# Block-balanced attention into expert routing: another layout for the block balancing, another order for the first loads

## The chip, the cores and the metric

The kernel runs on one core of one Trainium2 chip. The metric is the device time of one execution in microseconds (us).

## The reference, cut to what matters

Two layers are computed one after the other. The first is attention on 4 batches of 8 heads, with 768 positions of 64 numbers. For each batch and head an 8 by 8 matrix is balanced (five times: exponential, rows divided by their sums, columns divided by their sums), and the eight blocks of 96 keys and values are mixed with it before each block of queries attends to its block.

```python
P = sort_net                                   # 4, 8, 8, 8
for _ in range(5):
    P = P - np.max(P, axis=-1, keepdims=True)
    P = np.exp(P)
    P = P / (np.sum(P, axis=-1, keepdims=True) + 1e-09)
    P = P / (np.sum(P, axis=-2, keepdims=True) + 1e-09)
k_sorted = np.einsum('bhij,bhjcd->bhicd', P, k_b)
v_sorted = np.einsum('bhij,bhjcd->bhicd', P, v_b)
...                                            # softmax(q k^T / 8) v, block by block
x = attn_out                                   # 3072 rows of 512
# second layer: all 8 experts for every row, weighted by a balanced 3072 by 8 matrix
P = np.exp(x @ w_gate - max); 8 times: rows and columns divided by their sums
out += P[:, e:e + 1] * (np.maximum(x @ w1[e], 0.0) @ w2[e])    # for e in 0..7
```

## The kernel before, in words

The kernel is written in a framework that derives the waits from the data and may reorder instructions of an engine; an instruction wrapped in `pin` keeps its place behind everything that was written before it for its engine. All TensorE work is pinned, and so are nearly all loads, which GpSimd issues (`load_batch`, `load_rest` L67 to L77, `load_w1`, `load_w2`), since they convert f32 into bf16. These loads go through one queue in their order.

The first stage is the subject here. The 32 matrices lie on 32 partitions as P, 64 numbers each (L59). The balancing (L108 to L124) runs on VectorE alone, but for the exponentials on ScalarE. The result is written 16 times over as Prep (L126), turned by eight products with an identity into Pb (L352 to L354), and multiplied by a mask into R (`build_r`, L136): one 128 by 128 matrix per head, with which TensorE mixes the blocks. `sort_values` (L149) does this for the values of a batch and then exchanges partitions: eight DMAs (four issued by SP, four by GpSimd, L159 to L163) copy `vs` to `vsb`.

Loads are issued in this order: the first batch by halves (queries, values, keys of heads 0 to 3, then of heads 4 to 7, L94), the router's weights, the second batch's values (L97), then the four exchange pieces of GpSimd, and, behind a small copy that waits until the exchange has landed (`held`, L361 to L367), the first expert's weights w1 and w2 and the second batch's keys and queries.

`attention(bb, ...)` (L263) goes through a plan of steps: q queries are transposed, k keys mixed, s scores and their exponentials, m the mix with the values, t the output turned, l the router's logits, v one part (two heads) of the next batch's values, and wN N products that nothing reads (`warm`, L341). The digit is the pair of heads. For batch 0 the queries of pairs 0 and 1 are transposed before the balancing is done (L347). PSUM has seven banks in turn for all of this.

After batch 0, `attention` of the next batch is woven with `expert0` of the batch before (L385 to L409); twelve steps of the expert stand ahead of batch 1's attention (L388 to L390). Behind the last batch come the other seven experts, about 550 us of the span, which the change does not touch.

Of the kernel before, what the change touches and what calls it, by code (L numbers as in the profile page):

```python
# [13 lines left out]
F32 = mybir.dt.float32  # L14
BF16 = mybir.dt.bfloat16
AF = mybir.ActivationFunctionType
AX = mybir.AxisListType
ALU = mybir.AluOpType


def mkap(t, dims, off=0):
    return bass.AP(tensor=t.tensor, offset=t.offset + off, ap=dims)
# [3 lines left out]
def kernel(  # L26
# [11 lines left out]
    nc = tc.nc  # L38
# [17 lines left out]
    sp = actx.enter_context(tc.tile_pool(name="sp", bufs=3))  # L56


    P = pp.tile([32, 8, 8], F32)  # L59
    nc.sync.dma_start(out=P, in_=sort_net.rearrange("b h i j -> (b h) i j"))  # L60

    pin = tc.keep_in_program_order
    kt, vt, qt = {}, {}, {}
# [1 line left out]
    def load_batch(bb, parts):  # L67
        for d, name in ((vt, "vt"), (kt, "kt"), (qt, "qt")):
            d[bb] = kvp.tile([128, 8, 384], BF16, name=name, bufs=2)
        load_rest(bb, parts)  # L70
# [11 lines left out]
    def load_w1(e):  # L82
        w1t[e] = wp.tile([128, 4, F], BF16, name="w1e")
        pin(nc.gpsimd.dma_start(out=w1t[e],
                                in_=moe_w1[e].rearrange("(kk k) f -> k kk f", k=128)))
# [5 lines left out]

    Ibig = ones.tile([128, 128], BF16)
    make_identity(nc, Ibig)
    load_batch(0, [(x, l0, 4) for l0 in (0, 4) for x in "qvk"])  # L94
    wg = ones.tile([128, 4, E], BF16)
    nc.gpsimd.dma_start(out=wg, in_=moe_w_gate.rearrange("(kk k) e -> k kk e", k=128))
    load_batch(1, [("v", 0, 8)])  # L97
    mask16 = ones.tile([128, 16], F32)
    nc.vector.reduce_sum(out=mask16, in_=Ibig.rearrange("p (j c) -> p c j", c=16), axis=AX.X)

    VW = NB * 520
    vsbt = [perp.tile([128, VW], BF16, name=f"vsb{n}") for n in range(2)]
    vs = vsp.tile([128, 6, 8, 65], BF16)
    nc.vector.memset(vs[:, :, :, 64:65], 1.0)

    rs = pp.tile([32, 8], F32)  # L108
    cs = pp.tile([32, 8], F32)
    Pt = P.rearrange("p i j -> p j i")  # L110
    nc.vector.reduce_max(out=rs, in_=P, axis=AX.X)
    nc.vector.tensor_sub(P, P, mkap(rs, [rs.ap[0], rs.ap[1], [0, 8]]))
    for it in range(5):


        nc.scalar.activation(out=P, in_=P, func=AF.Exp)
        nc.vector.reduce_sum(out=rs, in_=P, axis=AX.X)
        nc.vector.reciprocal(out=rs, in_=rs)
        nc.vector.tensor_mul(P, P, mkap(rs, [rs.ap[0], rs.ap[1], [0, 8]]))
        nc.vector.reduce_sum(out=cs, in_=Pt, axis=AX.X)  # L120
        if it == 0:
            nc.vector.tensor_scalar_add(cs, cs, 1e-9)
        nc.vector.reciprocal(out=cs, in_=cs)
        nc.vector.tensor_mul(Pt, Pt, mkap(cs, [cs.ap[0], cs.ap[1], [0, 8]]))  # L124

    Prep = perp.tile([32, 8, 8, 16], BF16)  # L126
    for eng, i0 in ((nc.vector.tensor_copy, 0), (nc.scalar.copy, 4)):
        eng(Prep[:, i0:i0 + 4], mkap(P, [P.ap[0], [8, 4], [1, 8], [0, 16]], off=i0 * 8))

    xtT = xtp.tile([128, 4, N], BF16)  # L130
    osbl = xtp.tile([128, NT, Dm], F32)
# [1 line left out]
    Pb = perp.tile([128, 32, 8], F32)  # L133
    Rt = {}

    def build_r(bb, eng, n):  # L136

        Rt[bb] = perp.tile([128, 8, 8, 16], BF16, name=f"R{bb % 2}")
        for h in range(0, 8, n):
            ins = eng.tensor_tensor(  # L140
                out=mkap(Rt[bb], [Rt[bb].ap[0], [16, 8 * n], [1, 16]], off=h * 128),
                in0=mkap(Pb, [Pb.ap[0], [1, 8 * n], [0, 16]], off=(bb * 8 + h) * 8),
                in1=mkap(mask16, [mask16.ap[0], [0, 8 * n], [1, 16]]),
                op=ALU.mult)
            if eng is nc.gpsimd:
                pin(ins)


    def sort_values(bb, bank):  # L149
        for h in range(8):  # L150
            vps = bank([128, 384], F32)
            pin(nc.tensor.matmul(vps, Rt[bb][:, h].rearrange("p i c -> p (i c)"),
                                 vt[bb][:, h, :], start=True, stop=True))
            (nc.vector.tensor_copy if bb == 0 and h % 2 else nc.scalar.copy)(
                vs[:, :, h, 0:64], vps.rearrange("p (kk d) -> p kk d", d=64))
            if h % 2:
                yield

        for i in range(NB):  # L159
            eng = nc.gpsimd if i % 2 else nc.sync  # L160
            (pin if bb == 0 else lambda ins: ins)(eng.dma_start(
                out=mkap(vsbt[bb % 2], [[VW, 96], [1, 520]], off=i * 520),
                in_=vs[16 * i:16 * i + 16].rearrange("p kk h d -> p kk (h d)")))  # L163
# [3 lines left out]
    def queries(bb, hp, bank):  # L167

        qps = bank([128, 6, 128], BF16)
        if bb < 2:  # L170

            for kk in range(6):
                for h in range(2):
                    pin(nc.tensor.matmul(qps[64 * h:64 * h + 64, kk, :],
                                         qt[bb][:, 2 * hp + h, kk * 64:kk * 64 + 64],
                                         Ibig, is_transpose=True, start=True, stop=True))
        else:
            qr = sp.tile([128, 6, 2, 64], BF16, name="qr", bufs=2)
            nc.gpsimd.tensor_copy(
                qr.rearrange("p kk h d -> p h kk d"),  # L180
                qt[bb][:, 2 * hp:2 * hp + 2].rearrange("p h (kk d) -> p h kk d", d=64))
            for kk in range(6):
                pin(nc.tensor.matmul(qps[:, kk, :], qr[:, kk].rearrange("p h d -> p (h d)"),
                                     Ibig, is_transpose=True, start=True, stop=True))
        qT[bb, hp] = sp.tile([128, 128, 6], BF16, name="qTs", bufs=4)
        nc.scalar.copy(qT[bb, hp], qps.rearrange("p kk c -> p c kk"))
# [76 lines left out]
    def attention(bb, bank, values=None, warm=None):  # L263
        first = bb == 0

        def step(what, hp):
            if what == "q":
                queries(bb, hp, bank)
            elif what == "k":
                keys(bb, hp, bank)  # L270
            elif what == "s":
                scores(bb, hp, bank)
            elif what == "t":
                turn(bb, hp, bank, nc.scalar.copy if first else nc.vector.tensor_copy)
            elif what == "l":
                logits(bb, bank, (0, 1, 2) if hp == 0 else (3,))
            elif what == "v":
                next(values, 0)
            elif what == "w":
                warm(hp)  # L280
            else:
                for h in range(2):
                    mix(bb, hp, h, bank)

        plan = ("k0 k1 w4 s0 q2 k2 w2 s1 q3 k3 w3 s2 w4 s3 w3 m0 w3 m1 t0 v0 w3 m2 t1 v0 w3 "
                "m3 t2 v0 v0 w3 t3 l0 w3 l3 v0" if first else
                "q0,q1,k0 k1,s0,q2 k2,s1,q3 m0 k3,s2 m1,t0 s3 m2,t1 m3 t2 t3,l0 l3")
        for some in plan.split():
            for x in some.split(","):
                step(x[0], int(x[1]))  # L290
            yield
# [43 lines left out]
    with tc.tile_pool(name="ps0", bufs=7, space=bass.MemoryType.PSUM,  # L335
                      reuse_waits="tile") as ps0, \
            tc.tile_pool(name="psw", bufs=1, space=bass.MemoryType.PSUM) as psw:
        bank0 = lambda shape, dt: ps0.tile(shape, dt, name="bank", tag="bank")
        unread = psw.tile([128, 4, 128], F32)

        def warm(n):  # L341

            for _ in range(n):
                pin(nc.tensor.matmul(unread, Ibig, mkap(Ibig, [Ibig.ap[0], [0, 4], [1, 128]]),
                                     start=True, stop=True))

        for hp in range(2):  # L347
            queries(0, hp, bank0)
        warm(9)
        pbps = bank0([128, 8, 32], F32)  # L350
        for i in range(8):
            pin(nc.tensor.matmul(pbps[:, i, :], Prep[:, i].rearrange("p j c -> p (j c)"),  # L352
                                 Ibig[0:32, 0:32], start=True, stop=True))
        nc.vector.tensor_copy(Pb, pbps.rearrange("p i g -> p g i"))  # L354
        build_r(0, nc.vector, 2)
        warm(4)
        for _ in sort_values(0, bank0):
            pass
        build_r(1, nc.gpsimd, 4)

        held = pp.tile([96, 2], BF16)  # L361
        gate = nc.gpsimd.tensor_copy(
            held, mkap(vsbt[0], [[VW, 96], [520, 2]], off=6 * 520 + 519))
        with tc.issue_after(gate.ins):
            load_w1(0)
            load_w2(0)
            load_rest(1, [(x, l0, 4) for l0 in (0, 4) for x in "kq"])  # L367
        for _ in attention(0, bank0, sort_values(1, bank0), warm):
            pass

# [424 lines left out]
```

## Time and profile before

| | |
|---|---|
| three runs | 685.52 to 685.59 us, median 685.56 us |
| profiled execution | 686.2 us; span from first to last instruction 684.4 us |
| granted TensorE clock, mean | 0.997 |
| PE busy | 658.6 us (96% of the span) |
| VectorE, ScalarE, GpSimd busy | 473.4, 375.4, 444.3 us |
| read from HBM, written | 52.45 MB, 6.29 MB |

In lines of the profile, PE is TensorE, PEld its weight loads, DVE VectorE, ACT ScalarE, POOL GpSimd, SP SyncE. A timeline line has the start in us, the duration in us, the engine, the line of the kernel, the operation with the names of the tiles written and read, shapes, the number of instructions merged, and in brackets how long the engine had been idle and what it waited for. A line by stretches has the stretch, then the busy time of PE, PEld, DVE, ACT and POOL with instruction counts in brackets, the granted clock, the DMA share and the GB/s that the DMA engines wrote. A line of the chain of waits has the start, the duration and what ran.

### The profile page before, as it was taken

What the parts mean: (1) busy time and instruction counts of PE and PEld (TensorE: products, weight loads), DVE (VectorE), ACT (ScalarE), POOL (GpSimd) and SP (SyncE); (2) the same over time, 40 slices, a digit from 0 to 9 for tenths busy, and PEclk for the clock granted to TensorE, in tenths of its full rate; (3) what the DMA queues carried; (4) which work ended last, traced back from release to release, by engine and by line L of the source; (5) the groups of instructions that cost most, each with busy time, mean ns of one, the idle gap of its engine ahead of it and who ended that gap; (6) DMA issues with size and microseconds to landing.
All of it is one profiled execution on the core that took longest, in us unless ns stands there. A gap on an engine that the chain in (4) does not pass through costs nothing.

```text
span 684.4 us, 13128 instructions
## 1 busy us (share of the span) xinstructions
PE 658.6 (96%) x5011; PEld 428.7 (63%) x5088; DVE 473.4 (69%) x977; ACT 375.4 (55%) x725; POOL 444.3 (65%) x417
## 2 busy tenths in 40 slices
PE   5989999999999999999999999999999999999996
PEld 2646666644446666666666666666666666666665
DVE  6627555578656777777777777777777777777775
ACT  3746646345667765555555555555555555555540
POOL 4542324201929888959797887879796979846640
PEclk9999999999999999999999999999999999999998
DMA  9898833403040304030303021030403040000223
GB/s 147 167 215 127 142 75 63 63 0 62 0 63 1 62 1 62 2 62 1 62 2 57 6 39 24 4 61 1 63 1 61 1 62 1 2 1 36 88 100 148
DMA packets 31904, 36.57 MB, mean 53 GB/s; under 512 B 2016, under 2 KB 24288, under 8 KB 31840
## 3 DMA queue, kind: packets, MB, share of 16 engines
q0 software_dynamic: 26400, 27.82, 25.4%
q1 hardware_dynamic: 5440, 7.90, 3.4%
q8 instruction: 40, 0.66, 0.4%
q14 instruction: 24, 0.20, 0.1%
HBM read 52.45 MB, written 6.29 MB: 86 GB/s over the span
## 4 chain that ended last, share of the span: by engine, by line
PE 87%; DVE 5%; DMA 4%; issue 2%; ACT 1%; POOL 1%; SPq 0%; DVEq 0%; ACTq 0%; POOLq 0%
PE oacc L631 35%; PE bk L508 34%; PE bank L306 4%; PE bank L299 4%; DMA qt<-in_q_dram 3%; PE oacc L597 2%; PE bank L232 1%; PE bk L597 1%; DVE hT L497 1%; DMA vsb<-vs 1%; PE bank L215 1%; PE bank L196 1%; PE bank L243 1%; DVE cs L484 0%; PE bk L299 0%
## 5 line engine op out<-in xcount | busy, mean ns | idle before, releaser
L581 DVE SCALAR_TENSOR_TENSOR osbl<-oacc,glog,osbl 128x256 f32<-128x256 f32 (+1 forms) x398 | 214.6, 540 | 131.8 <-PE oacc L631 114.0
L494 ACT ACTIVATE hT<-bk 128x512 bf16<-128x512 f32 x162 | 96.7, 597 | 143.1 <-PE bk L508 133.2
L508 PE MATMUL bk<-xtT,w1e 128*128 128x512 bf16 x478 | 144.3, 379 | 1.9 <-ACT hT L494 0.7
L631 PEld LDWEIGHTS <-hs 128*128 128x128 bf16 x936 | 91.6, 98 | 59.8 <-issue 0.3
L621 POOL TENSOR_TENSOR hs<-hT 128x512 bf16<-128x512 bf16 x78 | 90.5, 1160 | 48.8 <-DVE hT L497 43.3
L631 PEld LDWEIGHTS <-hT 128*128 128x128 bf16 x860 | 84.1, 98 | 55.9 <-issue 1.5
L631 PE MATMUL oacc<-w2e,hT 128*128 128x256 bf16 x752 | 112.8, 273 | 1.4 <-DVE osbl L581 1.0
L631 PE MATMUL oacc<-w2e,hs 128*128 128x256 bf16 x648 | 97.2, 273 | 0.6
L508 PE MATMUL bk<-xc,wc 128*128 128x512 bf16 x319 | 96.3, 379 | 0.0
L621 POOL TENSOR_TENSOR hs<-hT,hs 128x512 bf16<-128x512 bf16 x78 | 90.0, 1154 | 6.1
L621 POOL TENSOR_TENSOR hs<-hs,hT 128x512 bf16<-128x512 bf16 x78 | 90.0, 1154 | 6.1
L508 PEld LDWEIGHTS <-w1e 128*128 128x128 bf16 x672 | 65.8, 98 | 18.4 <-issue 4.6
L497 DVE CUSTOM_DVE_ANT_0 hT<-bk,p 128x512 bf16<-128x512 f32 x90 | 62.2, 691 | 10.2 <-PE bk L508 3.0
L553 ACT COPY p<-bk 128x512 f32<-128x512 f32 x84 | 49.2, 585 | 26.6 <-PE bk L508 23.9
L547 ACT COPY u<-bk 128x512 f32<-128x512 f32 x84 | 49.2, 586 | 24.8 <-PE bk L508 22.3
L497 DVE CUSTOM_DVE_ANT_0 hT<-bk,u 128x512 bf16<-128x512 f32 x84 | 57.1, 680 | 0.0
L508 PEld LDWEIGHTS <-wc 128*128 128x128 bf16 x504 | 49.3, 98 | 10.8 <-issue 0.2
L530 ACT COPY bk<-bk 128x512 f32<-128x512 f32 x78 | 44.5, 571 | 19.9 <-PE bk L508 19.9
L571 DVE SCALAR_TENSOR_TENSOR s<-bk,hT 128x512 bf16<-128x512 f32 x78 | 53.1, 681 | 0.0
L508 PE MATMUL bk<-xc,w1e 128*128 128x512 bf16 x159 | 48.0, 379 | 1.7 <-DVE hT L497 1.6
L508 PE MATMUL bk<-xtT,wc 128*128 128x512 bf16 x159 | 48.0, 379 | 0.5
L444 POOL TENSOR_TENSOR w2e<-w2e 128x512 bf16<-128x512 bf16 x32 | 36.8, 1162 | 15.9 <-PE oacc L306 6.8
(120 smaller groups left out, 869.7 us busy)
## 6 DMA issues: line engine op xcount, KB each, us to landing
w1e<-in_moe_w_dram POOLq DMA_DIRECT2D x8, 1024.0 KB, 8.0
w2e<-in_moe_w_dram POOLq DMA_DIRECT2D x8, 1024.0 KB, 8.8
out_dram<-osbl SPq DMA_DIRECT2D x23, 256.0 KB, 2.0
vt<-in_v_dram POOLq DMA_DIRECT2D x3, 768.0 KB, 10.9
vsb<-vs SPq DMA_DIRECT2D x16, 97.5 KB, 5.1
vsb<-vs POOLq DMA_DIRECT2D x16, 97.5 KB, 4.7
qt<-in_q_dram POOLq DMA_DIRECT2D x4, 384.0 KB, 12.9
kt<-in_k_dram POOLq DMA_DIRECT2D x4, 384.0 KB, 13.5
```

The source lines that it names most:

```text
L299: hold(nc.tensor.matmul(hps[:, 0:n], w1t[e][:, kk, fb * 128:(fb + 1) * 128], xtT[:, kk, c0:c0 + n], start=(kk == 0), stop=(kk == 3)))
L444: pin(nc.gpsimd.tensor_tensor(out=c, in0=a, in1=b, op=ALU.subtract))
L494: relu = lambda o, x: nc.scalar.activation(out=o, in_=x, func=AF.Relu)
L497: return nc.vector._custom_dve(TENSOR_ADD_SAT, out=o, in0=x, in1=y, s0=TOP, s1=0.0)
L508: hold(nc.tensor.matmul(ps, wa[:, kk, :], xa[:, kk, :], start=(first and kk == 0), stop=(kk == 1), skip_group_check=True))
L530: hold(nc.scalar.copy(t["w"], t["u"]))
L547: hold(nc.scalar.copy(t["u2"], t["u"]))
L553: hold(nc.scalar.copy(t["p5"], t["v"]))
L571: hold(nc.vector.scalar_tensor_tensor(out=s3[:, i, :], in0=t["w"], scalar=0.0, in1=c12, op0=ALU.max, op1=ALU.subtract))
L581: pin(nc.vector.scalar_tensor_tensor(out=o, in0=ps, scalar=glog[:, t, e:e + 1], in1=o, op0=ALU.mult, op1=ALU.add))
L621: pin(nc.gpsimd.tensor_tensor(out=s[:, c], in0=a, in1=b, op=o))
L631: pin(nc.tensor.matmul(ps, h[:, fb, :], w[:, fb, :], start=(first and fb == 0), stop=(fb == 3), skip_group_check=True))
```

## The change

The matrices are laid out with one row per partition: two tiles of 128 partitions by 8 numbers, each with two batches. The row sum comes with the exponential (`accum_out`); the column sum is a product on TensorE with a 128 by 128 matrix of ones in blocks of eight (`group`), which is made from the identity. Only the first of the five steps subtracts the maximum, through the exponential's bias. The two halves are generators that take turns, with two `warm` products per turn. The last column division writes the 16-fold copy, `spread` turns it with one product, and the first batch's R is built straight from PSUM; the second half is finished behind the first batch's values.

Loads: the first batch comes as values, keys, queries; then the router's weights, now pinned. The second batch's values are loaded behind w1, and GpSimd's R for the second batch stands between them and w2. `held` and its wait are gone. In batch 0's plan the queries of pairs 0 and 1 come behind the keys, the parts of `v` are placed later, and there are 18 warm products instead of 31; around the balancing there are 16 in place of 13.

```diff
-    P = pp.tile([32, 8, 8], F32)
-    nc.sync.dma_start(out=P, in_=sort_net.rearrange("b h i j -> (b h) i j"))
+    Pg = [pp.tile([128, 8], F32, name=f"P{g}") for g in range(2)]
+    for g in range(2):
+        nc.sync.dma_start(out=Pg[g], in_=sort_net[2 * g:2 * g + 2].rearrange(
+            "b h i j -> (b h i) j"))
...
-    load_batch(0, [(x, l0, 4) for l0 in (0, 4) for x in "qvk"])
+    load_batch(0, [(x, l0, 4) for x in "vkq" for l0 in (0, 4)])
     wg = ones.tile([128, 4, E], BF16)
-    nc.gpsimd.dma_start(out=wg, in_=moe_w_gate.rearrange("(kk k) e -> k kk e", k=128))
-    load_batch(1, [("v", 0, 8)])
+    pin(nc.gpsimd.dma_start(out=wg, in_=moe_w_gate.rearrange("(kk k) e -> k kk e", k=128)))
...
+    mask8 = ones.tile([128, 16], F32)
+    nc.vector.reduce_sum(out=mask8, in_=Ibig.rearrange("p (g i) -> p g i", i=8), axis=AX.X)
+    group = perp.tile([128, 16, 8], F32)
+    nc.vector.tensor_copy(group, mkap(mask8, [mask8.ap[0], [1, 16], [0, 8]]))
...
+    def balance_blocks(g, bank):
+        P = Pg[g]
+        top, rs, cs = (pp.tile([128, n], F32, name=f"{x}{g}")
+                       for x, n in (("top", 1), ("rs", 1), ("cs", 8)))
+        nc.vector.reduce_max(out=top, in_=P, axis=AX.X, negate=True)
+        for it in range(5):
+            nc.scalar.activation(out=P, in_=P, func=AF.Exp, accum_out=rs,
+                                 **({"bias": top} if it == 0 else {}))
+            yield
+            nc.vector.reciprocal(out=rs, in_=rs)
+            nc.vector.tensor_scalar(out=P, in0=P, scalar1=rs, scalar2=None, op0=ALU.mult)
+            cps = bank([128, 8], F32)
+            pin(nc.tensor.matmul(cps, group.rearrange("p g i -> p (g i)"), P,
+                                 start=True, stop=True))
+            yield
+            if it == 0:
+                nc.vector.tensor_scalar_add(cs, cps, 1e-9)
+                nc.vector.reciprocal(out=cs, in_=cs)
+            else:
+                nc.vector.reciprocal(out=cs, in_=cps)
+            if it < 4:
+                nc.vector.tensor_mul(P, P, cs)
+            else:
+                nc.vector.tensor_tensor(
+                    out=Prep[g], in0=mkap(P, [P.ap[0], [1, 8], [0, 16]]),
+                    in1=mkap(cs, [cs.ap[0], [1, 8], [0, 16]]), op=ALU.mult)
+            yield
...
-        plan = ("k0 k1 w4 s0 q2 k2 w2 s1 q3 k3 w3 s2 w4 s3 w3 m0 w3 m1 t0 v0 w3 m2 t1 v0 w3 "
-                "m3 t2 v0 v0 w3 t3 l0 w3 l3 v0" if first else
+        plan = ("k0 k1 q0 q1 w2 s0 k2 q2 w2 s1 k3 q3 w2 s2 w2 s3 w2 m0 w2 m1 t0 w2 "
+                "m2 t1 v0 w2 m3 v0 t2 v0 w2 t3 l0 v0 l3 v0" if first else
...
-        for hp in range(2):
-            queries(0, hp, bank0)
-        warm(9)
-        pbps = bank0([128, 8, 32], F32)
-        for i in range(8):
-            pin(nc.tensor.matmul(pbps[:, i, :], Prep[:, i].rearrange("p j c -> p (j c)"),
-                                 Ibig[0:32, 0:32], start=True, stop=True))
-        nc.vector.tensor_copy(Pb, pbps.rearrange("p i g -> p g i"))
-        build_r(0, nc.vector, 2)
         warm(4)
+        one, two = (balance_blocks(g, bank0) for g in range(2))
+        for it in range(5):
+            next(one)
+            if it:
+                next(two)
+            next(two)
+            next(one)
+            next(two)
+            warm(2)
+            next(one)
+
+        def spread(g):
+            pbps = bank0([128, 128], F32)
+            pin(nc.tensor.matmul(pbps, Prep[g].rearrange("p j c -> p (j c)"), Ibig,
+                                 start=True, stop=True))
+            return pbps
+
+        pbps = spread(0)
+        build_r(0, nc.vector, 2, pbps)
+        nc.scalar.copy(Pb[:, 0:16], pbps.rearrange("p (g i) -> p g i", i=8))
+        warm(2)
         for _ in sort_values(0, bank0):
             pass
+        load_w1(0)
+        load_batch(1, [("v", 0, 8)])
         build_r(1, nc.gpsimd, 4)
-
-        held = pp.tile([96, 2], BF16)
-        gate = nc.gpsimd.tensor_copy(
-            held, mkap(vsbt[0], [[VW, 96], [520, 2]], off=6 * 520 + 519))
-        with tc.issue_after(gate.ins):
-            load_w1(0)
-            load_w2(0)
-            load_rest(1, [(x, l0, 4) for l0 in (0, 4) for x in "kq"])
+        load_w2(0)
+        load_rest(1, [(x, l0, 4) for l0 in (0, 4) for x in "kq"])
+        next(two)
+        nc.vector.tensor_copy(Pb[:, 16:32], spread(1).rearrange("p (g i) -> p g i", i=8))
```

More of the change, by code (lines that the diff above doesn't have):

```diff
@@ L106 @@
     nc.vector.memset(vs[:, :, :, 64:65], 1.0)
[L108 to L124, printed above, removed]
@@ L126 @@
-    Prep = perp.tile([32, 8, 8, 16], BF16)
-    for eng, i0 in ((nc.vector.tensor_copy, 0), (nc.scalar.copy, 4)):
-        eng(Prep[:, i0:i0 + 4], mkap(P, [P.ap[0], [8, 4], [1, 8], [0, 16]], off=i0 * 8))
+    Prep = [perp.tile([128, 8, 16], BF16, name=f"Prep{g}") for g in range(2)]
+    def balance_blocks(g, bank):
[25 more added lines that the diff above has]
+            yield
@@ L134, with build_r @@
     Rt = {}
-    def build_r(bb, eng, n):
+    def build_r(bb, eng, n, src=Pb):
         Rt[bb] = perp.tile([128, 8, 8, 16], BF16, name=f"R{bb % 2}")
@@ L141, in build_r @@
                 out=mkap(Rt[bb], [Rt[bb].ap[0], [16, 8 * n], [1, 16]], off=h * 128),
-                in0=mkap(Pb, [Pb.ap[0], [1, 8 * n], [0, 16]], off=(bb * 8 + h) * 8),
+                in0=mkap(src, [src.ap[0], [1, 8 * n], [0, 16]], off=(bb * 8 + h) * 8),
                 in1=mkap(mask16, [mask16.ap[0], [0, 8 * n], [1, 16]]),
```

## The prediction

> **What bounds the kernel now.** I read the page first (PE busy 96% of the span, so only stretches where PE lacks useful work can give time), then the busy time by 5 us stretches, the chain of waits, the DMA view of the first 60 us, and the timeline by engine. Busy share by stretch: from 50 us on PE is full, and before that it is not.
>
> ```profile
> 35.00:40.00 5.00, 5.00 (x37) 3.03 (x34) 0.21 (x1) 3.19 (x7) 0.98 (x2) 1.00 1.18 190
> 40.00:45.00 5.00, 3.76 (x18) 1.57 (x16) 1.38 (x2) 0.73 (x2) 1.42 (x2) 1.00 1.29 219
> 45.00:50.00 5.00, 3.94 (x82) 2.80 (x84) 2.10 (x4) 3.40 (x7) 3.58 (x4) 1.00 1.26 239
> 50.00:55.00 5.00, 5.00 (x96) 3.51 (x95) 3.79 (x12) 3.71 (x9) 0.26 (x1) 1.00 1.32 205
> ```
>
> The chain of waits, in order of time, says what sets the time at which PE becomes full: the load of batch 1's queries, not the balancing.
>
> ```profile
> 0.75 1.57 DMA P<-in_sort_net_dram
> ...
> 13.66 1.43 DVE R L140 x4
> 15.09 1.87 DVE vs L154 x4
> ...
> 19.06 5.42 DMA vsb<-vs
> 25.10 0.83 POOL w1e L84
> ...
> 29.02 19.95 DMA qt<-in_q_dram
> ```
>
> The DMA view of 0 to 60 us (40 slices of 1.5 us) shows the loads running at 201 to 208 GB/s, with a hole at 22.5 to 27 us (74, 11, 22): the hold keeps the weights back until the exchange has landed.
>
> ```profile
> GB/s 0 6 13 153 201 202 205 201 203 202 203 203 205 287 293 74 11 22 120 205 208 201 192 201 167 186 232 241 206 203 202 273 255 204 204 206 204 203 204 193
> ```
>
> The PE timeline behind batch 0's attention: twelve steps of expert 0 (L299, L306), then batch 1, which waits twice for queries.
>
> ```profile
> 34.83 0.31 PE L257 MATMUL bank<-wg,xtT 128*128 128x8 bf16 x6 [0.39 <-ACT xtT L246]
> 35.00 5.36 PE L299 MATMUL bank<-xtT,w1e 128*128 128x384 bf16 x32
> 40.20 3.62 PE L306 MATMUL bank<-w2e,hTs 128*128 128x512 bf16 x15
> 45.08 0.86 PE L174 MATMUL bank<-Ibig,qt 128*64 128x128 bf16 x24 [1.26 <-DMA qt<-in_q_dram]
> ...
> 49.01 0.53 PE L174 MATMUL bank<-Ibig,qt 128*64 128x128 bf16 x12 [0.83 <-DMA qt<-in_q_dram]
> ```
>
> So attention(0) ends at T0 = 35.0, and batch 1's third transposition of queries (call it Q) starts at 49.01. The work between needs 12.0 us: 8.8 for the twelve steps (35.00 to 43.82) and 3.2 from the first transposes to 48.2. Only 2 us are waits. If PE is as full after Q as now, the change is worth 49.0 minus the new Q, and new Q is T0 + 12.0 unless the queries come later.
>
> **Part by part.**
>
> *Balancing.* Removed per iteration: six small DVE operations and an exponential, 1.81 us (the multiplication starts at 4.53 and at 6.34). New, for one of two half-problems: exponential 0.29 (0.26 in L116, plus the hop), then two small DVE operations of 0.2, a product on TensorE, and two more DVE operations (0.45). The nearest row for the product is the router's balancing: reduction ends at 141.12, the next DVE operation starts at 141.61.
>
> ```profile
> 140.63 0.49 DVE L484 TENSOR_REDUCE cs<-glog 128x8 f32<-128x192 f32 x1
> 141.61 0.17 DVE L487 TENSOR_SCALAR cs<-bk 128x8 f32<-128x8 f32 x1 [0.48 <-PE bk L486]
> ```
>
> That is 0.48 for the hop through PE, so 1.65 alone; the other half's DVE work lies in the waits but for some 0.15, giving 1.8. The sum taken along in the exponential isn't in the trace: between nothing and another ACT instruction of 0.26. I take 0.1, near a small read-out: 1.9 per iteration. The first can start no earlier than now (same load of 1.57 us; TensorE also needs the group matrix, about 1 us of DVE work on the identity, and four warm products of up to 0.43, which cover each other), so the second exponential stays at 4.8 and the fifth is near 10.5 (now 10.43). Behind it now come 3.2 us to the first R (13.66): sums, a cast, eight products, a copy. New: about 2.7, since the cast falls into the last product, one matmul replaces eight, and R is built straight from PSUM. R starts at 13.2; bounds 12.4 (no read-out) to 14.4 (0.26 each, and PE at half speed). The second half's last two operations and its copy lie behind vs on DVE.
>
> *The exchange and the hold.* R to last vs copy takes 3.3 now (13.66 to 16.96); so 16.5. POOL issues four pieces, 0.5 us later and 0.53 each, until 19.1. The old value load of batch 1 no longer stands in front: batch 0's 2.36 MB (4 to 15.6 us at 0.203 MB/us) is through. The exchange lands near 23 (alone, at 95.4 to 101.7, it took 6.3 from the first issue), ahead of mix 0, which the order of PE puts at 24.4. Nothing waits for it in the old order either: 24.66 against a landing of 24.5.
>
> *Loads moved.* POOL's queue is now w1, v1, the two R operations (2.1), w2, keys and queries. Behind w1, v1 lands much later than now (20.4). w1: 8.3 from issue (L84's row), 27.4; v1 is 0.786 MB, 3.9 more: 31.3. R on POOL ahead of w2 is covered by 9 us of queued w1 and v1; without that cover it would cost 2.1. w2 at 36.5, the queries by 45.5 (1.57 MB, and 0.39 MB of batch 1's exchange beside them): 3.5 earlier than 49.0, and no longer the bound.
>
> *Queries 0 and 1 and the warm products.* The two transposes (0.9) and their copies on ACT (1.5) move behind the keys; six warm products fewer ahead of mix 0 (1.5) pay PE's part. ACT becomes the busy one: 4 copies of 0.8 and 16 exponentials of 0.41, 9.8 us from 16.8 to 26.6, as late as now (26.7). So mix 0 to turn 1 are done at about 29, as now (29.5).
>
> *The new wait.* The first v0 (values of batch 1) stands on PE behind turn 1, and v1 lands at 31.3. Queued behind it on PE: mix 3, turns 2 and 3, the logits and expert 0; who waits: DVE and ACT. From v1: v0 and w2 0.76, mix 3's DVE work from +1.1 to +3.0 (1.87 per head pair now), turn 3 to +3.45, its copy on ACT behind two pairs of vs copies and turn 2's until +4.5, the last logits: T0 = +4.85 = 36.15. Bounds of v1 30.4 to 32.2.
>
> Sum: Q = 36.15 + 12.0 = 48.15, against 49.01: -0.85, so about 0.8 us less. The hole in the loads is filled (-3.5), but most of it was hidden behind expert 0, and the late v1 gives 1.15 of the rest back.
>
> A row beside this: the warm products (L344) first take 0.39 each, nine in 3.5 us from 8.74; from 13.10 four take 1.04, so PE started slow and sped up near 11.6. The trace's longest pause of PE after 7.3, 43.82 to 45.08, did not slow what follows.
>
> ```profile
> 8.74 3.50 PE L344 MATMUL unread<-Ibig 128*128 128x512 bf16 x9
> 13.10 1.04 PE L344 MATMUL unread<-Ibig 128*128 128x512 bf16 x4
> ```
>
> [...]
>
> **Rivals.**
>
> 1. *v1 isn't late for PE* (it lands by 29.5, or balancing gains 1.5): attention(0) ends as now or at 34.7, Q = 47, -2.0: 683.6. For it: the hole is gone. Against it: 1.05 + 0.786 MB at 0.203 take 9 us, and w1 is issued near 19.
>
> 2. *The exchange shares the engines with the weights, and mix 0 waits for it.* Beside w2's stream batch 1's pieces take this long:
>
> ```profile
> DMA to landing us min/median/max: 6.7/8.5/15.0
> ```
>
> The last piece, issued at 18.6 to 19.1, would land at 27.6 instead of 23. From mix 0 to T0 are now 10.35 (24.66 to 35.0), so T0 = 38.0, Q = 50.0: +1.0, 686.5; with 10 us, 688. It is slower than before once the landing passes 26.65. Against it: the pieces are issued 2 us before w1 and stand ahead of it in POOL's queue; SP's share alone can be overtaken. [...]
>
> [...]
>
> 4. *The balancing does not gain:* a hop of 0.9 through a cold PE makes 2.3 per iteration; R at 14.9, everything 1.7 later: +0.9, 686.4.
>
> **How the numbers follow.** The profiled execution took 686.2 for a span of 684.4; the three times have the median 685.56, and I put the difference on that. Forecast 0.52: 684.8, its own range 683.9 to 685.9. Rival 1: 0.13; rival 2: 0.13; rival 3: 0.14; rival 4: 0.08. 0.2% is 1.37 us (684.2 to 686.9), about what a measurement of this kernel can tell from no change. Faster: rival 1 and a fifth of the forecast, 0.24. Slower: half of rival 2, a third of 3 and 4 each, and combinations of these, 0.23. The rest, 0.53, is within. The range 683.4 to 687.2 leaves out the late end of rival 2 and the early end of rival 1.
>
> **What would show it.** Right: exponentials 1.9 apart, R near 13.2; no hole in GB/s at 22 to 27; PE waiting at L152 for vt at 29 to 31; no wait for qt behind 45; Q near 48.1. Wrong: mix 0 waiting for vsb, warm products 0.43 apart behind 30, or PE waits behind Q that were not there before.

## The result, and the profile after

| | before | after |
|---|---|---|
| median | 685.58 us | 695.09 us (four runs, 692.71 to 696.33) |
| ratio to before | | 1.0133, interval 1.0106 to 1.0161 |
| profiled execution, its span | 686.2, 684.4 us | 692.71, 690.8 us |
| R for batch 0 starts | 13.66 us | 16.57 us |
| mix 0: first and last product | 24.66, 25.95 us | 27.91, 32.57 us |
| last logits of batch 0 end | 35.1 us | 43.6 us |
| third transposition of batch 1 (Q) | 49.01 us | 55.90 us |
| mean granted clock | 0.997 | 0.995 |

The change costs 9.5 us; I had forecast 0.8 less, in a range that ended at 687.2. The profiled execution is the quickest of the four. It is 6.4 us longer in span, and Q comes 6.9 later: the loss is made ahead of Q, and what follows is within 0.5 us of before.

Busy time by stretches of the changed kernel (columns as before: stretch, PE, PEld, DVE, ACT, POOL, granted clock, DMA share, GB/s). The column to look at is the clock, the third from the right; it is 1.00 in all these stretches before:

```profile
25.00:30.00 5.00, 3.25 (x48) 1.93 (x45) 0.87 (x3) 3.77 (x9) 5.00 (x7) 1.00 0.99 165
30.00:35.00 5.00, 3.16 (x35) 2.65 (x35) 2.75 (x13) 1.24 (x3) 0.58 (x1) 0.71 1.21 205
35.00:40.00 5.00, 5.00 (x51) 3.75 (x50) 3.11 (x14) 2.37 (x4) 0.00 (x0) 0.60 1.26 207
40.00:45.00 5.00, 3.94 (x55) 2.57 (x53) 1.61 (x7) 3.86 (x9) 0.65 (x2) 1.00 1.29 204
```

The PE timeline shows where this begins:

```profile
27.91 0.48 PE L241 MATMUL bank<-vsb,atp 96*96 96x65 bf16 x6
31.84 0.73 PE L241 MATMUL bank<-vsb,atp 96*96 96x65 bf16 x10 [3.45 <-DMA vsb<-vs]
...
33.22 1.46 PE L241 MATMUL bank<-vsb,atp 96*96 96x65 bf16 x16
...
39.16 0.88 PE L241 MATMUL bank<-vsb,atp 96*96 96x65 bf16 x16
...
44.11 5.36 PE L308 MATMUL bank<-xtT,w1e 128*128 128x384 bf16 x32 [0.48 <-ACT vs L163]
```

Mix 0 starts its first six products and then waits 3.45 us for the seventh block of the exchange. Behind the wait sixteen products take 1.46 us instead of 0.88; the full speed is back at 39. The chain of waits in order of time names the piece, the fourth that SP issues:

```profile
21.64 1.77 SPq L170
23.46 8.34 DMA vsb<-vs
31.84 0.73 PE bank L241 x10
```

SP's third issue took 1.77 us (SP's first four took 0.58 to 0.69 before), so the fourth was issued at 23.46, 0.5 us behind w1 (22.94), and landed 8.3 us later. The GB/s row (1.5 us slices) shows that the hole did not go; it moved to 16.5 to 21, since the first batch's loads end while the balancing is still running, and nothing else is queued:

```profile
GB/s 0 6 102 188 203 203 201 202 204 204 77 0 0 0 73 185 159 154 184 180 226 187 201 203 206 208 208 204 205 202 206 203 272 284 230 204 203 203 205 207
```

### The profile page after: what moved, and what is told of

It reads as the page before. It is cut to its first block, busy times and chain, and to the rows that moved or that the text cites. A ratio compares the mean times of both kernels' runs of the same rounds, so it can differ in the third digit from the quotient of the medians.

```text
span 690.8 us, 13241 instructions
## 1 busy us (share of the span) xinstructions
PE 670.8 (97%) x5092; PEld 434.0 (63%) x5092; DVE 473.1 (68%) x989; ACT 376.5 (55%) x740; POOL 443.9 (64%) x416
## 4 chain that ended last, share of the span: by engine, by line
PE 91%; DVE 5%; DMA 1%; ACT 1%; issue 1%; SPq 0%; DVEq 0%; ACTq 0%
PE bk L527 36%; PE oacc L650 35%; PE bank L308 5%; PE bank L315 5%; PE oacc L616 2%; PE bank L241 2%; DMA vsb<-vs 1%; PE bk L616 1%; DVE hT L516 1%; PE bank L224 1%; PE bank L252 1%; PE bank L205 1%; PE bank L123 1%; PE bank L161 1%; PE unread L353 1%
## 5 line engine op out<-in xcount | busy, mean ns | idle before, releaser
L527 PE MATMUL bk<-xtT,w1e 128*128 128x512 bf16 x504 | 149.9, 379 | 0.9 <-ACT hT L513 0.7
L527 PE MATMUL bk<-xc,wc 128*128 128x512 bf16 x336 | 99.9, 379 | 0.0
L527 PEld LDWEIGHTS <-w1e 128*128 128x128 bf16 x672 | 65.8, 98 | 18.6 <-issue 4.6
L527 PEld LDWEIGHTS <-wc 128*128 128x128 bf16 x504 | 49.3, 98 | 10.8 <-issue 0.2
L527 PE MATMUL bk<-xc,w1e 128*128 128x512 bf16 x168 | 49.9, 379 | 1.7 <-DVE hT L516 1.6
L527 PE MATMUL bk<-xtT,wc 128*128 128x512 bf16 x168 | 50.0, 379 | 0.0
```

What stands on the lines that cost most here:

```text
L527: hold(nc.tensor.matmul(ps, wa[:, kk, :], xa[:, kk, :], start=(first and kk == 0), stop=(kk == 1), skip_group_check=True))
```

## The experiments

Times are medians in us; the kernel before has 685.6 to 686.0 beside them, and a ratio is to that. Kernel 1 is the kernel of experiment 1, and so on; v1 stands for the second batch's values.

**1. Old loads and the hold, in the changed kernel.** Cut to what matters:

```diff
     pin(nc.gpsimd.dma_start(out=wg, ...))
+    load_batch(1, [("v", 0, 8)])
...
-        load_w1(0)
-        load_batch(1, [("v", 0, 8)])
         build_r(1, nc.gpsimd, 4)
-        load_w2(0)
-        load_rest(...)
+        held, gate = ...                       # as before
+        with tc.issue_after(gate.ins):
+            load_w1(0); load_w2(0); load_rest(...)
```

> The changed kernel, but with the second batch's values loaded right behind the router's weights, and w1, w2, keys and queries held behind the exchange, as before; the new balancing, plan and order v, k, q stay. Theory A (two separate losses: the balancing delays R by 2.9 us, and without the hold a piece of the exchange is overtaken by w1 and PE's clock falls in the wait): the exchange lands by 27, PE has no pause over 1.5 us, the clock stays full from some 18 us on, batch 0's attention ends near 37.5 and the third transposition of batch 1 starts near 51; 2 to 3 us over before, so 687.5 to 688.5. Rival B (the new balancing and plan cost nearly all of it): 5 us or more over before.

It takes 688.50 us, ratio 1.0039 (1.0024 to 1.0053): theory A. R starts at 16.56, mix 0 at 28.8 without a wait for the exchange, and Q at 51.70. So 6.6 of the 9.5 us lie in the later loads and the missing hold. The rest, 2.7, belongs to the new balancing, the plan and the order of the first loads together; R is 2.9 later.

**2. The kernel before, only without the hold.**

```diff
-        held = ...; gate = nc.gpsimd.tensor_copy(held, ...)
-        with tc.issue_after(gate.ins):
-            load_w1(0); load_w2(0); load_rest(...)
+        load_w1(0); load_w2(0); load_rest(...)
```

> The kernel before with only the hold taken out: w1, w2, keys and queries are issued right behind R for batch 1, near 21.9 us. Theory A (a piece is overtaken only if w1's packets begin while SP's pieces are still under way): the exchange lands between 25 and 27 instead of 24.5, the queries 2 us earlier than 49; the total within 1 us of before. Rival B (the hold is what protects the exchange): it lands at 28 or later, PE pauses over 3.4 us and runs at half clock after it; 3 us or more over before. Rival C (the hold only cost time): the exchange lands by 25, 1.5 to 2 us faster.

It takes 683.50 us, ratio 0.9964 (0.9952 to 0.9975); measured again in experiment 11, 683.52, 0.9969. Rival C, the hold only cost time, and 2.3 us of it instead of 1.5 to 2. The exchange lands at 24.7, mix 0 starts at 24.63 as before; the hole is one slice deep (112 GB/s), and PE has no wait for queries left:

```profile
43.72 0.86 PE L174 MATMUL bank<-Ibig,qt 128*64 128x128 bf16 x24
44.41 0.50 PE L196 MATMUL bank<-R,kt 128*64 128x128 bf16 x12
44.85 1.04 PE L306 MATMUL bank<-w2e,hTs 128*128 128x512 bf16 x4
45.82 0.53 PE L196 MATMUL bank<-R,kt 128*64 128x128 bf16 x12
46.27 0.56 PE L215 MATMUL bank<-qTs,kTs 64*96 64x96 bf16 x16
46.76 0.53 PE L174 MATMUL bank<-Ibig,qt 128*64 128x128 bf16 x12
```

Q moves from 49.01 to 46.76. This one deletion beats both kernels.

**3. The pause filled with warm products.** In the plan `s3 w2 m0` becomes `s3 w9 w9 m0`.

> The changed kernel with 18 warm products instead of 2 ahead of mix 0, 16 more of some 0.22 us, which fill PE's pause of 3.45 us and nothing else. Theory A (the pause halves the clock for 6.8 us, and that is on the path): the granted clock shows no half from 20 us on, batch 0's attention ends near 41 instead of 43.6; 2 to 3 us under the changed kernel, with less spread between its runs. Rival B (the half clock is hidden by VectorE and ScalarE): 0.5 us or less.

It takes 692.31 us (691.59 to 693.42), ratio 1.0093: 2.8 under the changed kernel's median, 1.1 between the profiled executions, and half the spread. The clock stayed full from 19.6 us on (the product of `spread` took 0.22 us at 19.65, as at full speed in the changed kernel); batch 0's attention ended at 42.7, not 41, because PE now reached the values first and waited for v1 from 36.01 to 37.48. So the slow clock is 1.1 to 2.8 us of the loss, and there is a second wait behind the first.

**4. The whole first exchange in GpSimd's queue.** `eng = nc.gpsimd if i % 2 or bb == 0 else nc.sync`.

> The changed kernel with all eight pieces of the first exchange issued by GpSimd, in the queue in which w1 follows. Theory A (SP's fourth piece, issued at 22, is overtaken by w1's packets of another queue): no piece can be overtaken now; the last is issued near 25 and lands by 28.5, PE's pause is under 1.5 us and the clock stays full; w1 and v1 come 2 us later, v1 near 37, so PE waits for v1 instead; attention(0) ends near 42, 1 to 2 us under the changed kernel. Rival B (the DMA engines are just busy): the last piece lands at 31 or later, and the total is no better.

It takes 694.54 us, ratio 1.0122: no better. The first half of theory A held: mix 0 runs from 28.17 to 29.46 without a wait for the exchange. The second half put v1 near 37, and it came at 39.3:

```profile
31.92 0.65 PE L252 MATMUL bank<-Ibig,og 96*128 96x96 bf16 x8
39.36 0.80 PE L161 MATMUL bank<-vt,R 128*128 128x384 bf16 x2 [6.79 <-DMA vt<-in_v_dram]
39.95 1.06 PE L353 MATMUL unread<-Ibig 128*128 128x512 bf16 x2
```

PE stands 6.8 us for v1, and two warm products behind it take 1.06 us, the slow clock's value. With v1 behind w1, mending the exchange alone is worth nothing here.

**5. The old balancing in the changed kernel.** P on 32 partitions, `balance_blocks` and `spread` out, the eight products and the copy back in, `warm(40)` under the balancing.

> The changed kernel with the balancing of before (32 partitions, VectorE alone), and 40 warm products under it instead of 14; loads, plan and the missing hold as changed. R for batch 0 should start near 13.7 us instead of 16.6, with the clock full. Theory A (the loads are a loss of their own): the last exchange piece of SP, issued near 19, is still overtaken by w1, or, if it lands in time, PE waits for v1 until 32 to 34; a pause over 3 us, half clock behind it; 2.5 to 3.5 us under the changed kernel, and 3 us or more over before. Rival B (all goes back to the late R): within 1 us of before.

It takes 690.45 us, ratio 1.0071 (1.0054 to 1.0088): theory A, though 4.6 us under the changed kernel instead of 2.5 to 3.5. R starts at 13.81; so the loads, with the plan, lose 4.5 us even with R on time. SP's fourth piece was issued only 0.1 us ahead of w1, and PE waited for the exchange twice:

```profile
25.72 0.28 PE L226 MATMUL bank<-vsb,atp 96*96 96x65 bf16 x2 [1.18 <-DMA vsb<-vs]
28.08 0.93 PE L226 MATMUL bank<-vsb,atp 96*96 96x65 bf16 x10 [2.08 <-DMA vsb<-vs]
```

and ran at half clock behind it for much longer than in the changed kernel (second line: stretch 28.2 to 40, clock 0.50):

```profile
24.00:28.10 4.10, 0.84 (x9) 0.57 (x8) 0.18 (x1) 1.08 (x3) 3.51 (x5) 0.83 1.11 215
28.20:40.00 11.80, 11.56 (x96) 8.56 (x96) 7.34 (x31) 5.52 (x11) 0.00 (x0) 0.50 1.26 202
40.50:45.00 4.50, 3.91 (x49) 2.47 (x47) 0.21 (x1) 3.01 (x7) 2.31 (x5) 1.00 1.31 205
```

**6. Values early, R between the exchange and w1, no hold,** in the changed kernel:

```diff
     pin(nc.gpsimd.dma_start(out=wg, ...))
+    load_batch(1, [("v", 0, 8)])
...
-        load_w1(0)
-        load_batch(1, [("v", 0, 8)])
         build_r(1, nc.gpsimd, 4)
+        load_w1(0)
         load_w2(0)
```

> The changed kernel with the second batch's values loaded right behind the router's weights as before, and R for batch 1 issued between the exchange and w1 as before; no hold. Theory A (the late v1 and the overtaken exchange were 4 us or more, the rest is the balancing): no PE pause behind 6 us, mix 0 near 28.5, batch 0's attention ends near 38.4 as with the hold, and the 0.9 us of waiting for queries there is gone; 687 to 688, so 1.2 to 2 us over before. Rival B (without the hold the exchange is late in any order): a pause over 2 us ahead of mix 0 and 690 or more.

It takes 686.83 us, ratio 1.0017 (1.0007 to 1.0026): theory A. There is no wait for the exchange in mix 0 (28.42 to 29.71); v's products start at 32.65, the last logits end at 38.0, and Q starts at 50.26.

**7. The same with w1 ahead of R,** two lines exchanged.

> As the kernel with the early values and no hold, but w1 is issued ahead of R for batch 1, so 2.1 us earlier, right behind the exchange's pieces. Theory A (SP's last piece is overtaken when w1 follows at once): the exchange lands at 30 or later, PE pauses over 2 us ahead of mix 0 and the clock halves if that lasts 3 us; 2.5 us or more over the kernel with R in between. Rival B (v1 alone was late): no pause, the same time as with R in between.

It takes 690.0 us, ratio 1.0071 (1.0035 to 1.0106), with six runs from 687.89 to 695.59: three lie at 688, three between 692 and 696. The profiled one (691.99) has the wait, and the clock is half behind it:

```profile
27.91 0.42 PE L242 MATMUL bank<-vsb,atp 96*96 96x65 bf16 x6
31.35 0.59 PE L242 MATMUL bank<-vsb,atp 96*96 96x65 bf16 x10 [3.02 <-DMA vsb<-vs]
```

In kernel 6 the same place reads:

```profile
28.42 0.75 PE L242 MATMUL bank<-vsb,atp 96*96 96x65 bf16 x12
```

So with w1 issued at once SP's last piece can be overtaken (issued at 23.3 here, it took 8.0 us to land), and 2.1 us of R on GpSimd in between had kept it ahead. That the three quick runs at 688 are those in which the piece kept ahead fits their full granted clock (0.999 and 1.000, against 0.991 to 0.997 in the others), but only the one execution was traced.

**8. The late R, first attempt.** On kernel 6: an exponential of a constant as ScalarE's first instruction, and `pin` on the two `reduce_max`.

> As the kernel with the early values and no hold, and with the activation table asked for by an exponential of one constant at the start, and the balancing's first reduction behind the group matrix on VectorE. Theory A (1.15 us of the late R is the table load behind the matrices' arrival, 1 us the group matrix made behind the first row sums): the first product starts near 3.5 instead of 5.7, R near 14.4, and the total falls by 2.0 us, to 685 to 685.8. Rival B (the iterations, 2.15 us instead of 1.81, are the whole loss): under 0.7 us less.

It takes 686.06 us, 0.8 less than kernel 6, near rival B's bound of 0.7; R came only 0.35 us earlier. The table was loaded at 0.74, but the pin did not bring the group matrix forward; the first product came at 4.95 instead of 5.73, and R at 16.26.

**9. VectorE's order kept.** On kernel 8: `pin` on the masks, the group matrix, the memset and every VectorE instruction of `balance_blocks`.

> As the kernel with the early activation table (early values, no hold), and with VectorE's balancing instructions kept in the order in which they are written: group matrix first, and each half's column division ahead of the other half's reciprocal. Theory A (the late R is VectorE's order: the group matrix behind the row sums, and one half's multiplication behind the other half's product): first product near 3.5, 1.9 us per iteration, R near 13.4 instead of 16.3; the total falls by 2.8 us, to some 683.2. Rival B (the two products of 1.02 us on a slow PE set the 2.15 us): R near 14.4, 1.8 us less.

R at 13.58, as theory A had it, but 684.56 (ratio 0.9984, 0.9975 to 0.9994), 1.5 less and not 2.8. In the trace mix 0 starts no earlier than in kernel 8 (27.84 against 27.74), and PE shows where the 2.7 us of R went: `spread(1)` now waits for the second half's last division, which the pins had put behind the copies of vs, and PE is slow for longer. The mixing of the values took 2.85 us instead of 2.25, and the keys and queries behind it 1.49 each instead of 0.91 and 0.86.

```profile
14.19 2.85 PE L165 MATMUL bank<-vt,R 128*128 128x384 bf16 x8
18.14 0.29 PE L374 MATMUL bank<-Ibig,Prep 128*128 128x128 bf16 x1 [1.09 <-DVE Prep L138]
```

**10. A third warm product per turn.** `warm(3)` for `warm(2)` in the balancing of kernel 9.

> The same with three warm products per turn instead of two. Theory A (PE's clock is half until 18 to 20 us because the balancing leaves it idle too long): the clock is full before 12 us, the products take 0.8 us per turn or less, R comes 0.3 us earlier and the mixing of the values 0.5 us sooner; 0.5 us or more under the kernel with two. Rival B (on a slow PE the third one pushes the next product back): R later by 0.5 us or more, and no gain.

It takes 684.47 us (ratio 0.9974, 0.9965 to 0.9982). Both effects are there: R is 0.5 later (14.12), and PE is at full speed from 14.8, where kernel 9 still takes 1.49 us for the keys at 18.36 (0.86 here), with the mixing of the values 2.00 us long instead of 2.85; Q starts at 47.60 against 49.07. Between the medians 0.1 us is left; the profiled execution of kernel 9 (685.35) is one of its longer ones, that of kernel 10 (683.89) one of its shorter.

**11. The kernel before without the hold, again, beside those two.**

> The kernel before without the hold again, beside the two others on one chip: 683.5 us, 2.3 us under before. If the kernel with VectorE's order kept is as fast as this, the new balancing is worth as much as the old one, and no more.

It takes 683.52 us. The new balancing in its written order, kernels 9 and 10, was still 1 us behind.

**12. The second half's end ahead of R.** `next(two)` moves up to `spread(0)`, on kernel 10.

> The kernel with VectorE's order kept and three warm products, with the second half's last division done ahead of R instead of behind the copies of vs. In the kernel without this TensorE stood still from 16.7 to 17.9 us for it. Theory A (that wait is all that keeps the new balancing behind the old one): no pause there, mix 0 near 25.2 instead of 26.4, the third transposition of batch 1 near 46.5 instead of 47.6; 683.3, level with the kernel before without its hold (683.5). Rival B (ScalarE's copies of queries, now behind the keys, set mix 0): mix 0 stays near 26.3 and the time within 0.4 us of 684.5.

It takes 683.94 us, ratio 0.9965 (0.9951 to 0.9978). The pause is gone and mix 0 starts at 25.72 instead of 26.37, but Q stays, 47.56 against 47.60: batch 0's logits end 0.7 earlier, and expert 0 then waits 0.48 us for a copy of vs. So neither theory holds as it stands: the pause was not all that was left, and by the trace its end gained nothing. The time lies within the spread of the kernel before without its hold. A mended new balancing is about as good as the old one; nothing shows it to be better.

## Why the prediction was wrong

*What held.* The base: attention(0)'s end plus 12.0 gives Q. After: 43.63 + 0.48 (expert 0 waits for a copy of vs) + 11.8 = 55.90; kernel 2: expert 0 starts at 34.98, and 34.98 + 11.8 = 46.76. The 2 us of waits for queries were what the hole cost; kernel 2 shows them as 2.3.

*What failed, in order of its steps.* The step that turned a gain into a loss is the second: the sum had no wait for the exchange, and PE stood 3.45 us for it and ran at half clock for 6.8 us behind it.

1. *Balancing, R at 13.2 (12.4 to 14.4)*: it was 16.57. The first exponential was to start no earlier than the old one (2.82), with the second at 4.8; they came at 3.70 and 7.25. The table load in front of the first one now waits for the matrices (it stood at 0.74 before):

```profile
2.40 1.28 ACT L117 ACT_TABLE_LOAD   x1 [2.40 <-DMA P<-in_sort_net_dram]
3.70 0.30 ACT L117 ACTIVATE P<-P,top 128x8 f32<-128x8 f32 x1
3.90 0.19 ACT L117 ACTIVATION_READ_ACCUMULATOR P<-P,top 128x1 f32 x1
```

That the exponential now reads the loaded tile itself is a likely reason and not shown; kernel 8 shows that an exponential of a constant ahead of it brings the table load back to 0.74. The group matrix, which I had hidden under the first exponential, stood behind the row sums on VectorE (5.40), and the first product came at 5.68. The read-out of the sum is a second instruction of 0.19 that starts 0.1 to 0.2 behind the first one's start, and the next starts 0.1 behind it: my 0.1 was about right. An iteration took 2.15 instead of 1.9, and VectorE's rows say why:

```profile
10.86 0.21 DVE L130 RECIPROCAL cs<-bank 128x8 f32<-128x8 f32 x1 [0.36 <-PE bank L123]
11.29 0.21 DVE L130 RECIPROCAL cs<-bank 128x8 f32<-128x8 f32 x1 [0.22 <-PE bank L123]
11.41 0.28 DVE L132 TENSOR_TENSOR P<-P,cs 128x8 f32<-128x8 f32 x2
```

The second half's reciprocal stands ahead of the first half's multiplication and waits for the second product; the halves run in step instead of in turn. The group matrix and the iteration both came from reading the written order as the order on an engine whose instructions are not pinned. Kernel 9, with that order and the early table load, has the first product at 3.54, 1.9 to 2.2 from one product to the next, and R at 13.58: the sum itself was good. Rival 4 had put a late R (14.9) on a slow PE; but in kernel 9 PE is as slow, two warm products taking 1.01 us there too, and R is on time; so a slow PE alone does not make R late.

2. *The exchange lands near 23, ahead of w1.* Rival 2 was right, and priced too low (landing at 27.6, chance 0.13): 31.8. Its "issued 2 us before w1" does not follow from the prediction's own times, which have the last piece at 18.6 to 19.1 and w1 at 27.4 - 8.3 = 19.1; and it took SP to issue every 0.6 us. In the traces SP's issue of its fourth piece started 0.5 us behind w1 to 0.1 ahead of it in the changed kernel and in kernels 3, 5 and 7, and the piece took 6.9 to 8.3 us to land; in kernels 2, 6 and 8 to 12 it started 1.1 to 2.7 us ahead, and took 3.5 to 6.0. With the landing at 31.84, rival 2's own sum gives Q at 31.84 + 10.35 + 12.0 = 54.2; the 1.7 us that are left to 55.90 are of the size of the slow clock (step 4).

3. *v1 at 31.3.* w1 was issued at 22.94, 3.8 later than I had it; from there to v1's landing (issued 23.72, 13.9 to landing) I had 12.2 and it took 14.7, since w1 took 10.8 beside the exchange instead of 8.3. In the changed kernel this stayed hidden behind the exchange; kernel 4 shows it bare, a wait of 6.8 us. Nor could the hole be filled by the prediction's own times: the first batch is through at 15.6, and w1 follows at 19.1. One sum beside it is off, without a consequence: 1.57 and 0.39 MB at 0.203 take 9.7 us and not 9, so the queries were due by 46.2.

4. *The clock.* Rival 3, a slow clock behind PE's wait for v1, had 0.14 and a price of 1 to 2; it came as well, behind the wait for the exchange. No run shows the term that it rests on, how long PE may pause before its clock falls; the chance and the third of it that the sum counts as slower were my estimate. What the runs showed in its place: 1.26 us in the kernel before did not slow what follows, and behind 3.45 us in the changed kernel PE ran at half clock for 6.8 us, which kernel 3 prices at 1.1 to 2.8.

The rivals were priced one by one on top of the forecast, and their chances add up to 1 with the forecast's; the "combinations of these" have no price of their own. But rivals 2 and 3 hang together: the 3.45 us that PE waits for the exchange are the pause behind which its clock is half. Their cause is not the late R: kernel 5, with R on time, has both. It is w1 issued right behind the exchange: kernel 7, with v1 early, has both in its trace, and kernel 6, with R in between, has neither.

Step by step from the kernel before to the changed one: no hold -2.3 (kernel 2), new balancing with its plan and order of the first loads +3.3 (kernel 6 less kernel 2), w1 at once and v1 behind it +8.3 (changed kernel less kernel 6). How the last splits between w1 and v1 is open, since kernel 7's median (690.0) lies between two groups of runs. In the traces with the late exchange v1 behind w1 adds little, Q at 55.90 in the changed kernel against 55.39 in kernel 7.

*Open.* Why one issue of SP takes 1.77 us. SP's four issues together, by its timeline, take 4.52 us in the changed kernel, 4.21 in kernel 12, 3.7 to 3.8 in kernels 1, 3, 5 and 7, 3.24 in kernel 6 and 2.77 in kernel 2; what stretches them stays open. It does not need w1: in kernel 1 the third issue took 1.57 us, and w1 came only at 27.9. And the 2.4 us between the profiled execution and the changed kernel's median: two of the three longer runs have a mean granted clock of 0.990, but left no trace.

## What to carry to other kernels

Before a step is costed as hidden or taking turns, check whether the order that the kernel is written in is the order on the engine; where instructions are not pinned, price both orders. A transfer that must arrive soon needs its distance to the next large load counted in queue time, with a reserve (SP's fourth piece took 3.5 to 6.0 us when issued 1.1 us or more ahead of w1, and 6.9 to 8.3 from 0.1 us ahead on), and a load that is moved behind another arrives later by the whole of that one: in the changed kernel w1 took 10.8 us, and v1, issued 0.8 us behind it, 13.9; in kernel 4 that is a wait of 6.8 us, where the hold had cost 2.3. Rivals that share a cause are added, not taken one at a time, and the range goes to their sum.

## What the runs showed of the hardware

The clock fell without one long pause: in kernel 5 pauses of 1.18 and 2.08 us, with two small products between them, were enough, where 1.26 us alone in the kernel before were not. Worked back from the mean of 0.83 over 24.0 to 28.1 us, it fell at 26.7, 0.7 us into the second pause; from the start of the first, at 24.54, to there PE had been busy for 0.28 of 2.2 us. Which pause brings the clock down the traces show only case by case: half clock behind 3.45 us in the changed kernel and behind 3.02 in kernel 7, full speed behind 1.26 in the kernel before and 1.47 in kernel 3. The pauses that the expectations of experiments 2 and 7 name with the half clock are no limits that a run shows. The clock stayed at half for 6.8 us in the changed kernel and, worked back in the same way from 0.97 over 40 to 45 us, for some 13.6 in kernel 5.

Nor did the new balancing's work bring the clock up: with the products and two warm ones per 2.15 us PE looks busy at half speed (idle for 0.26 to 0.50 us in a turn), yet in the changed kernel two warm products still took 1.01 at 15.41, and 0.61 at 21.05; the product of `spread` took 0.31 at 16.22 and 0.22 at 19.37. (The column of the granted clock reads 1.00 in these early stretches; here the slow clock is read from the durations alone.) One warm product more per turn brought the full speed forward: from kernel 9 to kernel 10 the first six products of the mixing went from 2.13 to 1.23 us, and the keys behind it from 1.49 to 0.86.

```profile
15.41 1.01 PE L353 MATMUL unread<-Ibig 128*128 128x512 bf16 x2
...
21.05 0.61 PE L353 MATMUL unread<-Ibig 128*128 128x512 bf16 x2
```
